# The first product of the second MoE by a seven-product scheme, for three pairs of f in its last pass

## Chip, cores and metric

One core of a Trainium2 chip runs one program that does all of the work: causal attention and two mixtures (here dense feed-forward layers, "MoE"). The metric is device time in microseconds for one execution. The core has five engines that run side by side, each taking its own instructions strictly in the order in which they were written: PE (TensorE, matrix products into PSUM), DVE (VectorE), ACT (ScalarE), POOL (GpSimd) and SP (which issues most DMAs). They wait for each other through semaphores.

## The reference, cut to what matters

```python
def reference(**kwargs):                       # S = 576, 4 batches, 8 heads of 64
    attn_out = _attn_ref(q, k, v, s)           # causal attention with a decay bias
    x = attn_out.transpose(0, 2, 1, 3).reshape(2304, 512)
    x = _moe_ref(x, w_in, w_out)               # relu(x @ w_in)**2 @ w_out
    return _moe2_ref(x, moe2_w_in, moe2_w_out)

def _moe2_ref(x, w_in, w_out):                 # x: 2304 x 512, w_in: 512 x 2048
    h = x @ w_in                               # the "first product"
    g = h * np.cos(h)
    return (g @ w_out).astype(np.float32)      # the "second product"
```

## The kernel before, in words

Everything is fp32 at the ends, and products are made from two-part numbers: each operand is split into a high part and a low part (high = the rounded value, low = what is left), and each product runs three passes (high with high, high with low, low with high; `PASSES`). Attention and the first MoE fill the first 597 us. The second MoE, which the change touches, is the rest.

The second MoE cuts the 2304 tokens into five blocks `j` (four of 512 tokens and one of 256) and the 2048 hidden columns into 16 slices `f` of 128. The loop at the end of the program goes over three passes `p` of slices, `GROUPS`: f 0 to 3, 4 to 8 and 9 to 15; in each pass over the blocks; in each block over the slices of the pass. One step (p, j, f) is called a chunk here. A chunk's work, with the helper that issues it:

- `m2_g1` (PE, L1371): the first product, 4 pieces of the 512 input columns times 3 passes = 12 matmuls of 512 columns (tokens) into one PSUM bank `hp`; each matmul has its own weight load.
- `m2_cos` (ACT L1383, then DVE L1384 and L1385): `a` = hp scaled to turns, `kf` = a rounded by adding and taking off a large number, less a.
- `m2_sin` (ACT L1392), `m2_mul` (DVE L1398: hp times the cosine), `m2_high` (ACT L1406: `gh`, the fp16 high part), `m2_rest` (L1413: `gl`, the low part; on POOL in the middle pass, on DVE otherwise).
- `m2_g2` (PE, L1426): the second product of the chunk two steps back (`G2LAG` = 2), 12 matmuls of 512 columns into four banks `o0` to `o3`. After the last slice of a pass the banks are evicted into `part`: two by DVE (L1433), two by ACT (`os`, L1438) with an addition on POOL (L1439).

The weights of the second MoE are prepared while the first two passes run: `w_clip` (ACT L804), `w_bits` (DVE L810, L814), `w_square` (ACT L847, for the scale), `w_hi` (ACT L829) and `w_lo` (DVE L838). In the middle pass one weight tile goes through per chunk, two are scaled and split in every second chunk. The tokens `y` lie in DRAM as `y_d`; `load_y` fetches 512 KB for 256 tokens. All of this is written in one fixed order per engine; nothing is reordered at run time.

Of the kernel before, what the change touches and what calls it, by code (L numbers as in the profile page):

```python
# [14 lines left out]
ALU = mybir.AluOpType  # L15
# [111 lines left out]
def attention_moe_moe_kernel(  # L127
# [679 lines left out]
    def w_bits(j):  # L807
# [8 lines left out]
        )  # L816
        yield

    def w_hi(j):
        m, f, a = wq[j]  # L820
        if m == 0:
# [6 lines left out]
        part[c] = t[:, 1]  # L828
        nc.scalar.activation(out=wt[m, f, a][:, 0], in_=wst[j][1], func=ACTF.Copy, scale=sm["wsc"][:, c:c + 1])  # L829

    def w_lo(j):
        m, f, a = wq[j]
        t, st = wt[wq[j]], wst.pop(j)[1]
# [8 lines left out]
    stat, part, sm = [], {}, {}  # L842

    def w_square(j):
        m, f, a = wq[j]
# [31 lines left out]
    def w_scale(f):  # L877

        c = slice(2 * f, 2 * f + 2)
        powers(stat[0][:, c], sm["wsm"][:, c], sm["wex"][:, c], sm["wsc"][:, c])  # L880
        for g, (f0, f1) in enumerate(GROUPS):
            if f == f1 - 1:
                group(g, f0, f1)

    def group(g, f0, f1):

        fs = slice(f0, f1)
        t, u = (sm["wsc"][:, 2 * f0 + a:2 * f1:2] for a in range(2))
        lo, il = (sm[x][:, g:g + 1] for x in ("wlo", "wil"))
        inverse(sm["win"][:, fs], t)  # L890
        nc.vector.tensor_tensor(out=sm["wtu"][:, fs], in0=t, in1=u, op=ALU.mult)
        inverse(sm["wiu"][:, fs], sm["wtu"][:, fs])
        nc.vector.tensor_reduce(out=lo, in_=sm["wtu"][:, fs], op=ALU.min, axis=mybir.AxisListType.X)
        inverse(il, lo)
        nc.vector.tensor_scalar(
            out=sm["gsc"][:, fs], in0=sm["wiu"][:, fs], scalar1=lo, scalar2=2.0 ** -16, op0=ALU.mult, op1=ALU.mult
        )
        known[0].append(g)
        for j0, j1 in known[1]:
            tables(g, j0, j1)  # L900
# [3 lines left out]
    def tables(g, j0, j1):  # L904

        fs = slice(*GROUPS[g])
        n, js = GROUPS[g][1] - GROUPS[g][0], slice(j0, j1)
        nc.vector.scalar_tensor_tensor(
            out=sm["hsc"][:, js, fs], in0=sm["win"][:, None, fs].to_broadcast([128, j1 - j0, n]),
            scalar=1.0 / (2.0 * math.pi), in1=sm["yin"][:, js, None].to_broadcast([128, j1 - j0, n]),  # L910
            op0=ALU.mult, op1=ALU.mult,
        )
        nc.vector.tensor_scalar(
            out=sm["osc"][:, g, js], in0=sm["yin"][:, js], scalar1=sm["wil"][:, g:g + 1], scalar2=2.0 ** 16,
            op0=ALU.mult, op1=ALU.mult,
        )

# [142 lines left out]
    def moe_slot():  # L1060
        part, n = slots.pop(0)
        k, f = chunks[n]
        if part == 1:
            w_need(spot[0, f, 0] + 1)
            g1(k, f)
            return n
        w_need(spot[0, f, 1] + 1)
        rests(n)
        g2(k, f)
        g2done[0] += 1  # L1070
        if k == NB1 - 1 and 2 * f >= RAWS:
            w_load(2 * (NF + f))
            w_load(2 * (NF + f) + 1)
            nw[0] = max(nw[0], 2 * (NF + f + 1))

    def act(n):
        if n is not None:
# [123 lines left out]
    def w_sums():  # L1201
        while wsum:
            m, f, a = wq[wsum[0]]
            sum_rows(2 * f + a, (sm["wss"], 2 * f + a))
            wnext.append(wsum.pop(0))

    def w_scales():
        while len(wnext) > 1:
            w_scale(wq[wnext[0]][1])
# [150 lines left out]
    hd2 = {}  # L1360
    ops = {}

    def m2_g1(j, f):
        n = blocks[j][1]
        yh, yl = yd[j]
        w = wt[1, f, 0]
        hp = ps2h.tile([128, n], F32, tag="h", bufs=3, name="hp2")
        m = 0
        for c in range(KD):
            for a, e in PASSES:  # L1370
                nc.tensor.matmul(  # L1371
                    hp, w[:, a, c * 128:(c + 1) * 128], (yh, yl)[e][:, c, :],
                    start=(m == 0), stop=(m == 3 * KD - 1),
                )
                m += 1
        hd2[j, f] = hp

    def m2_cos(j, f):
        n = blocks[j][1]
        hp = hd2[j, f]  # L1380
        a = p2.tile([128, n], F32, tag="a", bufs=2, name="a")
        kf = p2.tile([128, n], F32, tag="kf", bufs=2, name="kf")
        nc.scalar.activation(out=a, in_=hp, func=ACTF.Copy, scale=sm["hsc"][:, j, f:f + 1], bias=0.25)  # L1383
        nc.vector.tensor_scalar(out=kf, in0=a, scalar1=MAGIC, scalar2=None, op0=ALU.add)  # L1384
        nc.vector.scalar_tensor_tensor(  # L1385
            out=kf, in0=kf, scalar=MAGIC, in1=a, op0=ALU.subtract, op1=ALU.subtract
        )
        hd2[j, f] = (hp, a, kf)

    def m2_sin(j, f):  # L1390
# [57 lines left out]
    steps2 = [(p, j, f) for p, fs in enumerate(GROUPS) for j in range(NB2) for f in range(*fs)]  # L1448
    bits0 = nw[2]
    for i in range(len(steps2) + G2LAG):  # L1450
        new = i < len(steps2)
# [5 lines left out]
        if new:  # L1457
            p, j, f = steps2[i]
            w_stats(2 * NF + 2 * GROUPS[p][1])
            w_need(2 * NF + 2 * f + 2)  # L1460
            m2_g1(j, f)
            m2_cos(j, f)
        if i < G2LAG:
            m2_sin(j, f)
            m2_mul(p, j, f)
            m2_high(p, j, f)
            m2_rest(p, j, f)
        elif i <= len(steps2) and i > G2LAG:
# [81 lines left out]
```

## Time and profile before

| what | value |
|---|---|
| time, three runs | median 976.35 us (975.49 to 977.0) |
| profiled execution | span 975.0 us from first to last instruction; the runs lie 0.5 to 2.0 us above it |
| PE busy, whole span | 954.7 us (98%) |
| DVE / ACT / POOL busy | 714.3 / 656.2 / 161.9 us |
| second MoE | from about 597 us to the end |
| middle pass and last pass | about 691 to 807 us, and 807 to 971 us |

How to read it: a busy share of PE counts matmuls whose ends are modelled, so the spacing from one start to the next says more than the length of one. The same holds for DVE and ACT: an instruction's listed length reaches a little into the next one, so what a queue really spends on one is read from start to start.

### The profile page before, as it was taken

The numbers are of one execution on the slowest core, as the hardware profiler recorded it, in microseconds if no ns is written. First come the engines' busy times: TensorE is split into PE (matmuls) and PEld (weight loads), VectorE is DVE, ScalarE is ACT, GpSimd is POOL, SyncE is SP. The second block draws the span as 40 slices with busy tenths as digits, with TensorE's granted clock in tenths as the row PEclk, the third lists the DMA queues.
The fourth block names the chain that finished last, engine by engine and source line by source line (L and its number), as shares of the span: only waits on it lengthen the run. The fifth ranks groups of instructions, "written<-read, shape, count | busy, mean of one in ns | idle before, by whom it ended". The sixth has DMA issues, their size and how long they took to land.

```text
span 975.0 us, 20374 instructions
## 1 busy us (share of the span) xinstructions
PE 954.7 (98%) x7250; PEld 735.2 (75%) x7250; DVE 714.3 (73%) x1816; ACT 656.2 (67%) x1596; POOL 161.9 (17%) x251
## 2 busy tenths in 40 slices
PE   6999999999999999999999999999999999999998
PEld 5898899999999999999999996445544454444444
DVE  6899988778778777777996364888789865545555
ACT  6799877777778777776784686677558653334433
POOL 2000112111110111111110031440133430101101
PEclk9999999999999999999999999999999999999999
DMA  8974698658988865586996688200000000001101
GB/s 252 319 256 137 156 211 218 169 140 173 166 180 195 177 187 146 131 175 143 205 226 123 216 284 343 65 23 1 1 1 1 0 2 0 34 11 44 43 2 66
DMA packets 150518, 127.19 MB, mean 130 GB/s; under 512 B 107864, under 2 KB 125600, under 8 KB 150416
## 3 DMA queue, kind: packets, MB, share of 16 engines
q1 hardware_dynamic: 146512, 119.59, 47.7%
q0 software_dynamic: 3904, 6.30, 2.4%
q8 instruction: 57, 0.93, 0.4%
q14 instruction: 45, 0.37, 0.1%
HBM read 85.79 MB, written 15.83 MB: 104 GB/s over the span
## 4 chain that ended last, share of the span: by engine, by line
PE 84%; ACT 5%; DVE 5%; DMA 3%; issue 1%; POOL 1%; SPq 0%; DVEq 0%; ACTq 0%; POOLq 0%
PE hp L1371 19%; PE o L1426 19%; PE hps L942 18%; PE y L971 18%; PE qkp L557 5%; PE pvs L684 4%; DMA rw<-in_w_dram 2%; PE xps L739 1%; DVE wt L835 1%; ACT st L804 1%; ACT wt L823 1%; DVE sb L575 1%; ACT sb L598 1%; DMA v_d<-vt 0%; ACT g L954 0%
## 5 line engine op out<-in xcount | busy, mean ns | idle before, releaser
L942 PE MATMUL hps<-xh,wt 128*128 128x256 f32 x1152 | 238.9, 290 | 1.9 <-ACT g L953 1.7
L971 PE MATMUL y<-gh,wt 128*128 128x256 f32 x1152 | 236.4, 288 | 0.0
L942 PEld LDWEIGHTS hps<-xh,wt 128*128 128x128 f32 x1152 | 190.0, 192 | 4.2 <-ACT g L953 3.1
L971 PEld LDWEIGHTS y<-gh,wt 128*128 128x128 f32 x1152 | 188.8, 191 | 1.0
L1371 PE MATMUL hp<-yh,wt 128*128 128x512 f16 (+1 forms) x640 | 185.9, 358 | 0.0
L1426 PE MATMUL o<-wt,gh 128*128 128x512 f16 x576 | 171.3, 379 | 0.1
L942 PE MATMUL hps<-xl,wt 128*128 128x256 f32 x576 | 163.3, 284 | 0.2 <-DVE xl L756 0.2
L971 PE MATMUL y<-gl,wt 128*128 128x256 f32 x576 | 162.8, 283 | 0.1
L1371 PEld LDWEIGHTS <-wt 128*128 128x128 f16 x960 | 92.0, 98 | 93.0
L1383 ACT ACTIVATE a<-hp,hsc 128x512 f32<-128x512 f32 (+1 forms) x80 | 51.5, 644 | 111.3 <-PE hp L1371 109.5
L953 ACT ACTIVATE g<-hps 128x256 f32<-128x256 f32 x144 | 54.8, 380 | 102.1 <-PE hps L942 99.0
L1371 PE MATMUL hp<-yl,wt 128*128 128x512 f16 (+1 forms) x320 | 114.4, 358 | 0.0
L942 PEld LDWEIGHTS hps<-xl,wt 128*128 128x128 f32 x576 | 110.8, 192 | 0.7 <-DVE xl L756 0.4
L971 PEld LDWEIGHTS y<-gl,wt 128*128 128x128 f32 x576 | 110.1, 191 | 1.0 <-DVE gl L961 0.4
L1426 PE MATMUL o<-wt,gl 128*128 128x512 f16 x288 | 109.2, 379 | 0.0
L1426 PEld LDWEIGHTS <-gh 128*128 128x128 f16 x576 | 56.3, 98 | 64.6 <-ACT gh L1406 0.6
L1384 DVE TENSOR_SCALAR kf<-a 128x512 f32<-128x512 f32 (+1 forms) x80 | 35.7, 447 | 92.6 <-ACT a L1383 92.3
L383 POOL DMA_DIRECT2D k<-ext_d x80 | 41.1, 514 | 319.9 <-ACT g L954 102.3
L598 ACT ACTIVATE sb<-sb,nb 128x128 f32<-128x128 f32 (+7 forms) x152 | 87.6, 576 | 2.5 <-DVE nb L575 2.0
L1392 ACT ACTIVATE a<-kf 128x512 f32<-128x512 f32 (+1 forms) x80 | 46.8, 584 | 50.8 <-DVE kf L1385 50.7
L961 DVE TENSOR_TENSOR gl<-g,gh 128x256 fp32r<-128x256 f32 x144 | 60.1, 417 | 27.3 <-ACT gh L955 14.3
L575 DVE CUSTOM_DVE_ANT_0 sb<-qkp,mask 128x128 f32<-128x128 f32 (+7 forms) x152 | 69.2, 455 | 6.2 <-PE qkp L542 3.3
(124 smaller groups left out, 1681.9 us busy)
## 6 DMA issues: line engine op xcount, KB each, us to landing
rw<-in_w_dram SPq DMA_DIRECT2D x64, 512.0 KB
raw<-in_qk_dram SPq DMA_DIRECT2D x48, 352.0 KB
raw<-in_qk_dram SPq DMA_DIRECT2D x16, 384.0 KB
v_d<-vt SPq DMA_DIRECT2D x16, 320.0 KB
vb<-v_d SPq DMA_DIRECT2D x32, 160.0 KB
vr<-in_v_dram POOLq DMA_DIRECT2D x15, 320.0 KB, 5.0
y_d<-yst SPq DMA_DIRECT2D x18, 256.0 KB
yr<-y_d SPq DMA_DIRECT2D x9, 512.0 KB
```

What stands on the lines that cost most here:

```text
L383: nc.gpsimd.dma_start(out=hd[n][1][64:68, BT - nq:BT + nl], in_=ext_d[n, :, BT - nq:BT + nl])
L557: nc.tensor.matmul(p[0:r, 0:cn], m[0:kk, qo:qo + r], m[0:kk, BT + c0:BT + c0 + cn], start=(kk == 128 and not (two and h % 2)), stop=(kk == ...
L575: nc.vector.tensor_tensor_reduce(out=sb[0:r, c0:c0 + cn], in0=p[0:r, 0:cn], in1=mask[0:r, mo:mo + cn], scale=-0.125, scalar=(3.0e38 if k = ...
L598: nc.scalar.activation(out=sb[0:r, 0:w], in_=sb[0:r, 0:w], func=ACTF.Exp, scale=-1.0, bias=j["nb"], accum_out=z[0:r, ti, x:x + 1],)
L942: nc.tensor.matmul(hp, w[:, a, c * 128:(c + 1) * 128], (xh, xl)[e][:, c, :], start=(n == 0), stop=(n == 3 * KD - 1),)
L953: nc.scalar.activation(out=g, in_=hp, func=ACTF.Relu)
L961: nc.vector.tensor_tensor(out=gl, in0=g, in1=gh, op=ALU.subtract)
L971: nc.tensor.matmul(yps[k][d // 2][:, d % 2, :], w[:, a, d * 128:(d + 1) * 128], (gh, gl)[e], start=(f == 0 and n == 0 and d % 2 == 0), sto ...
L1371: nc.tensor.matmul(hp, w[:, a, c * 128:(c + 1) * 128], (yh, yl)[e][:, c, :], start=(m == 0), stop=(m == 3 * KD - 1),)
L1383: nc.scalar.activation(out=a, in_=hp, func=ACTF.Copy, scale=sm["hsc"][:, j, f:f + 1], bias=0.25)
L1392: nc.scalar.activation(out=a, in_=kf, func=ACTF.Sin, scale=-6.2831850)
L1426: nc.tensor.matmul(ops[j][a], (gh, gl)[e][:, a * 128:(a + 1) * 128], w[:, x, :], start=(first and m == 0), stop=(last and m == 2),)
```

## The change

In the last pass, for f from 10 on and the four blocks of 512 tokens, two slices f and f+1 are made together (a "unit"). The product of a 512 x 256 weight by 512 x 512 tokens is seen as a 2 by 2 by 2 product of halves (two halves of the input columns, two slices, two halves of the tokens), and instead of 8 half products it makes 7 (`PROD`), each of 2 pieces x 3 passes = 6 matmuls of 256 columns. Three PSUM banks hold running sums; what is in a bank between two products is copied out to `hs` in SBUF by ACT (`snap`) or added to `hs` by DVE (`join`).

The products need sums and differences of the operands. For the weights (`pair_high`) they are made once per pair when the weight is prepared, in the middle pass: four DVE operations on 256 columns, five pieces instead of two for high and for low parts. For the tokens (`t_make`) they are made per block, one step at each call of `t_tick`: the block is loaded from `y_d` again, four DVE differences of 512 columns, four highs on ACT, four lows on DVE. The first block's are made at the end of the middle pass (`T_FROM`), each later block's during the block before.

Besides, the rounding in `m2_cos` adds and subtracts the large number in one DVE operation and takes `a` off with a plain two-tensor operation, where before the second step did both; the order of loading the last weights follows the pairs; a scale constant is lowered by one power of two and the later factors raised to match. The block of 256 tokens and f = 9 are done as before.

```diff
+    def pair_high(j, m):
...
+        if m == 0:
+            q = p2q[0].tile([128, KD, BT], F32, tag="yr", bufs=2, name="sums")
+            x, y = (wst[j + n][1].rearrange("p (a c) -> p a c", a=2) for n in range(2))
+            for n, (u, v, op) in enumerate((
+                (y[:, 0], y[:, 1], ALU.add), (q[:, 0], x[:, 0], ALU.subtract), (x[:, 0], y[:, 0], ALU.subtract),
+                (x[:, 1], q[:, 1], ALU.subtract),
+            )):
+                nc.vector.tensor_tensor(out=q[:, n], in0=u, in1=v, op=op)
+            parts = ((t[:, :, 1:3], x), (t[:, :, 0], y[:, 1]), (t[:, :, 3], q[:, 0]))
...
+        else:
...
+            parts = ((t[:, :, 0:3], q[:, 1:4]), (t[:, :, 3], y[:, 0]))
...
+        for o, i in parts:
+            nc.scalar.activation(out=o[:, 0], in_=i, func=ACTF.Copy, scale=sc)
...
+            for o, i in parts:
+                nc.vector.scalar_tensor_tensor(
+                    out=o[:, 1], in0=i, scalar=sc, in1=o[:, 0], op0=ALU.mult, op1=ALU.subtract
+                )
...
-        nc.vector.tensor_scalar(out=kf, in0=a, scalar1=MAGIC, scalar2=None, op0=ALU.add)
-        nc.vector.scalar_tensor_tensor(
-            out=kf, in0=kf, scalar=MAGIC, in1=a, op0=ALU.subtract, op1=ALU.subtract
-        )
+        nc.vector.tensor_scalar(out=kf, in0=a, scalar1=MAGIC, scalar2=MAGIC, op0=ALU.add, op1=ALU.subtract)
+        nc.vector.tensor_tensor(out=kf, in0=kf, in1=a, op=ALU.subtract)
...
+    def unit(j, f, prev):
...
+        prod(j, f, 1, 0, True)
+        prod(j, f, 2, 1, True)
+        snap(j, f, 0, 0, 0)
+        join(j, f, 1, 0, 0)
+        out_part(first, 0)
+        for x in old:
+            m2_sin(*x[1:])
+        if old:
+            m2_mul(*old[0])
+        else:
+            m2_high(*prev[1:])
+            m2_rest(*prev[1:])
+        prod(j, f, 6, 0, False)
+        if old:
+            m2_high(*old[0])
+            m2_mul(*old[1])
+        snap(j, f, 0, 1, 0)
+        prod(j, f, 7, 2, True)
+        out_part(first, 1)
+        if old:
+            m2_high(*old[1])
+            m2_rest(*old[0])
+            m2_rest(*old[1])
+        prod(j, f, 5, 0, False)
+        snap(j, f, 0, 1, 1)
+        join(j, f, 2, 1, 1)
+        out_part(second, 0)
+        t_tick(j + 1)
+        prod(j, f, 3, 0, False)
+        snap(j, f, 0, 0, 1)
+        prod(j, f, 4, 2, False)
+        join(j, f, 2, 1, 0)
+        out_part(second, 1)
+        t_tick(j + 1)
+        for m in range(2):
+            m2_cos(j, f + m)
+            fifo.append((p, j, f + m))
```

`prod(j, f, x, b, start)` issues product x into bank b. `out_part` issues half of the second product of an earlier chunk; of the first unit in the first block there is only one such chunk (`first`), of every other unit two (`first`, `second`). `old` are the two slices of the unit before, whose cosine and split are finished inside this unit.

Three places where the order changes. The first is DVE's queue in the middle pass, where the weights of one pair are prepared. Before, after the rounding of a chunk (`kf`), the two weight tiles are finished, and then come the next tile's bits (`st`) and the chunk's own multiplication (L1398):

```order
L1385 SCALAR_TENSOR_TENSOR kf<-kf,a 128x512
L838 SCALAR_TENSOR_TENSOR wt_11405<-st,wsc,wt_11405 128x512
L838 SCALAR_TENSOR_TENSOR wt_11407<-st,wsc,wt_11407 128x512
L810 TENSOR_SCALAR st<-st 128x512
L814 SCALAR_TENSOR_TENSOR st<-rw,st 128x512
L1398 SCALAR_TENSOR_TENSOR a<-hp_11384,gsc,a 128x512
```

After the change the same place reads:

```order
L1439 TENSOR_TENSOR kf<-kf,a 128x512
L855 TENSOR_TENSOR sums<-st 128x256
L855 TENSOR_TENSOR sums<-sums,st 128x256
L855 TENSOR_TENSOR sums<-st 128x256
L855 TENSOR_TENSOR sums<-st,sums 128x256
L874 SCALAR_TENSOR_TENSOR wt_11407<-st,wsc,wt_11407 128x512
L874 SCALAR_TENSOR_TENSOR wt_11407<-st,wsc,wt_11407 128x256
L874 SCALAR_TENSOR_TENSOR wt_11407<-sums,wsc,wt_11407 128x256
L874 SCALAR_TENSOR_TENSOR wt_11416<-sums,wsc,wt_11416 128x768
L874 SCALAR_TENSOR_TENSOR wt_11416<-st,wsc,wt_11416 128x256
L813 TENSOR_SCALAR st<-st 128x512
L1450 SCALAR_TENSOR_TENSOR a<-hp_11386,gsc,a 128x512
```

Nine operations stand between `kf` and the bits, where there were two (the second bits operation, L817, stands between the last two rows shown). The second place is ACT's queue in the second unit of a block (here the second block): `hs<-bank` are the copies out of the running banks, `a<-hs` and `a<-kf` scale and sine, CAST the high part `gh`, `os` evictions, `wt<-wt` and `wt<-yr` the high parts for the next block's tokens.

```order
L1492 ACTIVATE os<-o_12342,osc 128x512 [waits PE_49]
L1520 ACTIVATE wt_9853<-wt_11300,ysc 128x512 [waits DVE_49]
L1437 ACTIVATE a<-hs,hsc 128x512 [waits Activation_49]
L1437 ACTIVATE a<-hs,hsc 128x512 [waits DVE_49]
L1581 COPY hs<-bank 128x256 [waits PE_49]
L1444 ACTIVATE a<-kf 128x512 [waits DVE_49,Activation_49] x2
L1458 CAST gh<-a 128x512 [waits DVE_49]
L1581 COPY hs<-bank 128x256 [waits PE_49]
L1458 CAST gh<-a 128x512 [waits DVE_49]
```

Before, ACT had no copies out of the banks at all in this pass; its rows for one chunk were three:

```order
L1383 ACTIVATE a<-hp_12723,hsc 128x512
L1406 CAST gh<-a 128x512
L1392 ACTIVATE a<-kf 128x512
L1383 ACTIVATE a<-hp_12763,hsc 128x512
L1406 CAST gh<-a 128x512
```

The copies now stand between the steps of the cosine, and PE waits for them. The third place is PE in that kind of unit: the first row of a product, with what it waits for (`wt_97..` and `wt_98..` right after the arrow are token tiles made by `t_make`).

```order
L1571 MATMUL bank<-wt_9719,wt_11623 128x256 [waits Activation_49]
L1571 MATMUL bank<-wt_9853,wt_11623 128x256 [waits DVE_49]
...
L1571 MATMUL bank<-wt_9717,wt_11614 128x256 [waits Activation_49]
L1480 MATMUL o_12310<-wt_11511,gh 128x512
L1480 LDWEIGHTS gl [waits DVE_49]
...
L1571 MATMUL bank<-yh,wt_11623 128x256 [waits Activation_49]
L1571 MATMUL bank<-wt_9855,wt_11614 128x256 [waits DVE_49]
```

Before, a chunk's twelve matmuls of the first product went one after the other into one bank without such waits.

## Rows read from the trace of the kernel before

**Rows 1.** Head of the page.
```profile
span 975.0 us, 20374 instructions
```

**Rows 2.** Busy time in one stretch: PE, PEld, DVE, ACT, POOL, granted clock, DMA.
```profile
737.00:747.00 10.00, 10.00 (x50) 4.53 (x48) 9.68 (x17) 8.10 (x16) 2.55 (x3) 1.00 0.00 1
```

**Rows 3.** Timeline of one chunk in the last pass: start, length, engine, line, operation [idle].
```profile
851.36 0.59 PE L1426 MATMUL o<-wt,gh 128*128 128x512 f16 x2
851.56 0.69 ACT L1383 ACTIVATE a<-hp,hsc 128x512 f32<-128x512 f32 x1 [1.43 <-PE hp L1371]
852.14 0.61 ACT L1406 CAST gh<-a 128x512 f16<-128x512 f32 x1
852.28 0.43 DVE L1384 TENSOR_SCALAR kf<-a 128x512 f32<-128x512 f32 x1 [1.45 <-ACT a L1383]
852.74 0.69 DVE L1385 SCALAR_TENSOR_TENSOR kf<-kf,a 128x512 f32<-128x512 f32 x1
853.35 0.68 DVE L1413 TENSOR_TENSOR gl<-a,gh 128x512 f16<-128x512 f32 x1
853.95 0.38 PE L1371 MATMUL hp<-yh,wt 128*128 128x512 f16 x1
```

**Rows 4.** Timeline of one chunk of the block of 256 tokens.
```profile
950.87 1.41 PEld L1371 LDWEIGHTS <-wt 128*128 128x128 f16 x12
951.09 0.27 PE L1371 MATMUL hp<-yh,wt 128*128 128x256 f16 x1
...
952.40 0.59 PE L1426 MATMUL o<-wt,gh 128*128 128x512 f16 x2
952.60 0.47 ACT L1383 ACTIVATE a<-hp,hsc 128x256 f32<-128x256 f32 x1 [1.85 <-PE hp L1371]
...
953.43 0.43 DVE L1385 SCALAR_TENSOR_TENSOR kf<-kf,a 128x256 f32<-128x256 f32 x1
...
953.77 0.42 DVE L1413 TENSOR_TENSOR gl<-a,gh 128x256 f16<-128x256 f32 x1
```

**Rows 5.** Timeline of DVE in the middle pass, where weights are split.
```profile
732.00 1.60 DVE L1385 SCALAR_TENSOR_TENSOR kf<-kf,a 128x512 f32<-128x512 f32 x1
733.53 1.40 DVE L838 SCALAR_TENSOR_TENSOR wt<-st,wsc,wt 128x512 f16<-128x512 f32 x2
...
736.08 0.75 DVE L1398 SCALAR_TENSOR_TENSOR a<-hp,gsc,a 128x512 f32<-128x512 f32 x1
...
763.25 1.64 DVE L838 SCALAR_TENSOR_TENSOR wt<-st,wsc,wt 128x512 f16<-128x512 f32 x2 [0.59 <-ACT wt L829]
...
771.92 0.43 DVE L1384 TENSOR_SCALAR kf<-a 128x512 f32<-128x512 f32 x1 [0.89 <-ACT a L1383]
```

**Rows 6.** Timeline of POOL there.
```profile
731.90 1.16 POOL L1413 TENSOR_TENSOR gl<-a,gh 128x512 f16<-128x512 f32 x1 [2.40 <-ACT gh L1406]
737.56 1.35 POOL L1413 TENSOR_TENSOR gl<-a,gh 128x512 f16<-128x512 f32 x1 [4.50 <-ACT gh L1406]
...
757.83 1.34 POOL L1413 TENSOR_TENSOR gl<-a,gh 128x512 f16<-128x512 f32 x1 [4.51 <-ACT gh L1406]
```

**Rows 7.** Timeline of PE there: the matmuls at three points where PE could wait.
```profile
740.14 0.38 PE L1426 MATMUL o<-wt,gl 128*128 128x512 f16 x1
...
760.96 0.38 PE L1426 MATMUL o<-wt,gl 128*128 128x512 f16 x1
...
776.79 0.59 PE L1426 MATMUL o<-wt,gh 128*128 128x512 f16 x2
```

**Rows 8.** Timeline of ACT at the third pair's place: highs, two evictions.
```profile
772.92 1.32 ACT L829 ACTIVATE wt<-st,wsc 128x512 f16<-128x512 f32 x2
...
774.66 1.25 ACT L1438 ACTIVATE os<-o,osc 128x512 f32<-128x512 f32 x2
```

**Rows 9.** Two DVE lines, 690 to 970 us: shortest/median/longest ns, span of starts.
```profile
L1385 DVE SCALAR_TENSOR_TENSOR kf<-kf,a x60: 424/692/1602, 691.7 to 967.8; 128x512 f32<-128x512 f32 x48, 128x256 f32<-128x256 f32 x12
L1398 DVE SCALAR_TENSOR_TENSOR a<-hp,gsc,a x61: 473/746/752, 690.3 to 968.7; 128x512 f32<-128x512 f32 x48, 128x256 f32<-128x256 f32 x13
```

More of the change, by code (lines that the diff above doesn't have):

```diff
@@ L817, in w_bits, with split @@
         yield
+    def split(j):
+        return wq[j][0] == 1 and wq[j][1] >= PAIR0 and wq[j][2] == 0
+    pair = {}
     def w_hi(j):
         m, f, a = wq[j]
+        if split(j):
+            pair_high(j, f % 2)
+            return
         if m == 0:
@@ L840, in w_lo @@
         )
-    stat, part, sm = [], {}, {}
+    stat, part, half, sm = [], {}, {}, {}
     def w_square(j):
@@ L1070, in moe_slot @@
         g2done[0] += 1
[L1071 to L1074, printed above, removed]
+        if k == NB1 - 1 and 2 * f >= RAWS and not (f >= PAIR0 and f % 2 == 0):
+            while nw[0] < 2 * (NF + f + 1):
+                w_load(nw[0])
+                nw[0] += 1
     def act(n):
@@ L1446, in m2_g2, with t_make, minus, high @@
                     nc.sync.dma_start(out=out[row:row + m, :], in_=part[4 * j + a][x:x + m])
-    steps2 = [(p, j, f) for p, fs in enumerate(GROUPS) for j in range(NB2) for f in range(*fs)]
-    bits0 = nw[2]
-    for i in range(len(steps2) + G2LAG):
-        new = i < len(steps2)
+    HB = BT
+    PROD = {1: (0, 1, 0), 2: (0, 2, 1), 3: (1, 2, 2), 4: (0, 0, 6), 5: (0, 3, 3), 6: (1, 0, 4), 7: (1, 1, 5)}
+    yt = {}
+    def t_make(j):
+        to = [half[4 * (j % 2) + x].bitcast(F16).rearrange("p (e c h) -> p e c h", e=2, c=2) for x in range(4)]
+        ysc = sm["ysc"][:, j:j + 1]
+        load_ys(j)
+        yield
+        r, q = (yr[j, a] for a in range(2))
+        t3 = part[18].rearrange("p (c h) -> p c h", c=2)
+        src = (r[:, 0:2], q[:, 2:4], t3, r[:, 2:4])
+        def minus(o, x, y):
+            nc.vector.tensor_tensor(out=o, in0=x, in1=y, op=ALU.subtract)
+        def high(x):
+            nc.scalar.activation(out=to[x][:, 0], in_=src[x], func=ACTF.Copy, scale=ysc)
+        def low(x):
+            nc.vector.scalar_tensor_tensor(
+                out=to[x][:, 1], in0=src[x], scalar=ysc, in1=to[x][:, 0], op0=ALU.mult, op1=ALU.subtract
+            )
+        minus(src[2], q[:, 2:4], q[:, 0:2])
+        yield
+        high(2)
+        minus(src[0], q[:, 0:2], r[:, 0:2])
+        yield
+        high(0)
+        low(2)
+        minus(src[1], q[:, 2:4], src[0])
+        yield
+        high(1)
+        low(0)
+        minus(src[3], r[:, 2:4], src[1])
+        yield
+        high(3)
+        low(1)
+        yield
+        low(3)
+        yt[j] = to
@@ new lines, in attention_moe_moe_kernel, with t_tick, y_side, prod @@
+    now2 = [0, t_make(0)]
+    def t_tick(j):
+        while now2[0] <= min(j, NB2 - 2):
+            if next(now2[1], now2) is not now2:
+                return
+            now2[0] += 1
+            now2[1] = t_make(now2[0])
+    def y_side(j, x, e, c):
+        if x < 3:
+            return yd[j][e][:, c + 2 * (x > 0), HB * (x == 2):HB * (x == 2) + HB]
+        return yt[j][x - 3][:, e, c]
+    bank = {}
+    def prod(j, f, x, b, start):
+        m, wx, yx = PROD[x]
+        w = pair[f][m]
+        if start:
+            bank[b] = ps2h.tile([128, 2 * HB], F32, tag="h", bufs=3, name="bank")
+        n = 0
+        for c in range(2):
+            for a, e in PASSES:
+                nc.tensor.matmul(
+                    bank[b][:, 0:HB], w[:, a, wx, c * 128:(c + 1) * 128], y_side(j, yx, e, c),
+                    start=(start and n == 0), stop=(n == 5), skip_group_check=True,
+                )
+                n += 1
@@ new lines, in piece, with snap, join, out_part @@
+    def piece(j, f, m, t):
+        return hd2[j, f + m][:, t * HB:(t + 1) * HB]
+    def snap(j, f, b, m, t):
+        nc.scalar.copy(piece(j, f, m, t), bank[b][:, 0:HB])
+    def join(j, f, b, m, t):
+        o = piece(j, f, m, t)
+        nc.vector.tensor_tensor(out=o, in0=bank[b][:, 0:HB], in1=o, op=ALU.add)
+    fifo = []
+    def out_part(x, n):
+        if x is not None:
+            k = blocks[x[1]][1] // 128 // 2
+            m2_g2(*x, pick=range(n * k, n * k + k))
+    def unit(j, f, prev):
+        p = len(GROUPS) - 1
+        w_need(2 * NF + 2 * f + 4)
+        while now2[0] <= j:
+            t_tick(j)
+        first = fifo.pop(0) if len(fifo) != 2 or prev[0] != "u" else None
+        second = fifo.pop(0) if len(fifo) > 1 else None
+        for m in range(2):
+            hd2[j, f + m] = stq[0][0].tile([128, 2 * HB], F32, tag="stg", bufs=4, name="hs")
+        old = [prev[1:], (prev[1], prev[2], prev[3] + 1)] if prev[0] == "u" else []
+        prod(j, f, 1, 0, True)
[32 more added lines that the diff above has]
+        t_tick(j + 1)
+        for m in range(2):
+            m2_cos(j, f + m)
+            fifo.append((p, j, f + m))
@@ L1452, in attention_moe_moe_kernel @@
+    bits0 = nw[2]
+    prev = None
+    for i, (kind, p, j, f) in enumerate(items):
+        if kind == "u":
+            unit(j, f, prev)
+            prev = (kind, p, j, f)
+            continue
         if i >= QUIET:
@@ L1500, in attention_moe_moe_kernel @@
             y_sums(NB2 - 1, NB2)
+        if i >= T_FROM:
+            t_tick(0 if p < 2 else j + 1)
+        fifo.append((p, j, f))
+        prev = (kind, p, j, f)
+    m2_high(*prev[1:])
+    m2_rest(*prev[1:])
+    while fifo:
+        m2_g2(*fifo.pop(0))
 def _lay_out(inputs):
```

128 lines of the change are left out of this document (83 added, 45 removed).

## The prediction, as it was put on record before the changed kernel was run

> **What bounds the kernel now.** I read the span first [rows 1], then the busy time by stretch, then the timeline of a chunk. The second MoE is bound by PE: in ten microseconds of its middle pass PE is busy for all ten, at the full granted clock of 2.4 GHz [rows 2], and in the last pass the twelve matmuls of a second product start at 851.36 and the next chunk's first at 853.95, that is 2.59/12 = 0.216 us from start to start [rows 3]. So a chunk costs PE 24 x 0.216 = 5.19 us, and what shortens PE's list shortens the kernel, as long as nothing makes PE wait. The reader should see a second thing in [rows 2]: DVE is at 9.68 of 10 us there. It is a hair from being the bound of the middle pass, and the change adds to it just there.
>
> **What the change takes away.** Twelve units (three pairs in four blocks) replace 24 matmuls of 512 columns by 42 of 256. The price of 256 columns is read in the last block: twelve start at 951.09, the next matmul at 952.40, so 1.31/12 = 0.109 us each [rows 4]. A unit's first product goes from 24 x 0.216 = 5.19 to 42 x 0.109 = 4.59 us. Saved: 0.60 us, times 12 = **7.2 us**, if PE never waits.
>
> **New waits in the last pass.** Durations are from start to start, which is shorter than the listed length: ACT on 512 columns 0.58, DVE `kf` 0.46 and 0.61 [rows 3]; DVE on 256 columns with two inputs 0.34 [rows 4]; a DVE eviction or low about 0.66 to 0.70, half of two in 1.40 [rows 5]. From PE's last start plus its column time to ACT's start is 0.20 us (952.40 plus nothing to 952.60, [rows 4]); I take 0.13 us from an ACT or DVE end to its reader. The copy of a bank (256 columns out of PSUM on ACT) is not in the trace: below it 0.33, half a 512-column step and a start cost, above it the 0.47 listed for L1383 [rows 4]; I take 0.37, the start-to-start value that the 512-column row suggests, and 0.40 for the addition from a bank on DVE (between 0.34 and 0.43).
>
> Three kinds of wait follow.
> - In the very first unit only one chunk is at hand for the second product, so product 3 follows product 5 into the same bank at once: 0.20 + 0.37 + 0.13 = 0.70 us.
> - In the second unit of blocks 1 and 2 the queues arrive late. The unit before has carried the evictions of the previous block and the first token differences. Counted from the start of product 1: ACT still has an eviction copy (0.20 to 0.79), a high part (to 1.39) and two scalings (to 2.55), so the copy of bank 0 ends at 2.92 and product 6, which could start at 2.61, starts at 3.05: 0.44. DVE can begin the four `kf` steps only with the first scaling (1.97 + 0.13, a POOL addition pushes it to 2.17) and ends them at 4.27, then a bank addition (4.67) and the first multiplication (5.28); ACT's CAST, 5.43 to 5.95, stands ahead of the copy of product 6, 5.95 to 6.32. Product 5 could start at 5.66 and starts at 6.45: 0.79. Together 1.23 in each of two blocks.
> - The second unit of block 0 (no eviction) 0.24, that of block 3 (no new tokens to make, but the POOL additions) 1.23, and 0.04 at one more start.
>
> Sum 0.70 + 2 x 1.23 + 0.24 + 1.23 + 0.04 = **4.7 us** back. From below only the 0.70 is certain; from above, with 0.05 more on each copy, addition and low, 5.3, and 6.5 if the third units wait as well. The third units run free in this table, since DVE has caught up by then.
>
> Part of that sum is a matter of ports. L1398 read the product from PSUM and never took over 752 ns in 61 runs; L1385, with both inputs in SBUF, took up to 1602 [rows 9], as at 732.00, while a POOL operation ran from 731.90 for 1.16 us [rows 5, 6]. With `hs` in SBUF the multiplication joins the second kind. I count 1.0 of the 4.7 us for waits behind the POOL additions. The Trainium skill (SBUF — State Buffer, "Who interferes with whom") says that a DVE instruction with two SBUF inputs contends with a GpSimd instruction that reads SBUF and one of the two blocks fully. The trace agrees (1602 against 752 ns); without the rule the waits would sum to 3.7.
>
> The new rounding I put at nothing: its second step, a two-tensor operation, occupies DVE like the one before (0.61 for L1385; L1413, also two SBUF inputs, is listed at 0.68 against 0.69, [rows 3]), and its first is one pass over the same columns. If the first step lost its speed it would take about 0.6 instead of 0.46, and then the middle pass would lose more (case D). The second loading of `y` is issued a whole chunk before its first reader and PE has 5.2 us of other work; I price it at nothing, and 1 to 2 us once if DVE stands waiting for the first block's.
>
> **New waits in the middle pass.** DVE's queue gets, per pair, four operations of 256 columns (4 x 0.34 = 1.36 us) and five lows in place of two. The two took 1.40 [rows 5]; the five are one of 512 (0.66), three of 256 (3 x 0.35) and one of 768 (0.9, the 512-column value plus half of it less the start), 2.6 together. Per pair 1.36 + 2.6 - 1.40 = 2.6 us more. ACT's five highs are 1.2 us more and wait for the sums; they lie beside DVE's lows. Everything queued behind on DVE comes later by 2.6 us: the next bits and the chunk's multiplication, hence CAST, POOL's `gl` and PE's second product.
> - First pair, at 733.53: POOL's `gl` runs 737.56 to 738.91, PE reads it at 740.14 [rows 6, 7]: 1.2 us of slack. 2.6 - 1.2 = 1.4 us of waiting.
> - Second pair, two chunks times two later: DVE has had no idle time in between (9.68 of 10, [rows 2]), so its lateness is 5.2 us. `gl` runs 757.83 to 759.17, PE reads it at 760.96: slack 1.8. PE is then 5.2 - 1.8 = 3.4 us late in all, so 2.0 more.
> - Third pair: DVE's idle 0.59 and 0.89 us [rows 5] bring its lateness down to about 3.7, near PE's own 3.4. Here ACT's eviction decides. It began at 774.66, and bank 1 was free at about 775.2, 1.6 us before PE's 776.79 [rows 7, 8]. Now it stands behind DVE's sums (1.36) and longer highs (1.2), with 0.1 for the hand-over, on a queue 0.2 later than PE: 2.9 - 1.6 = 1.3; `gl` behind the POOL additions loses no more. I take 1.1.
>
> Sum 1.4 + 2.0 + 1.1 = **4.5 us**. From below 0, if DVE's waits for POOL fall elsewhere (the 0.9 us that L1385 lost at 732.00 recurs at most chunks) and free the 2.6 us; from above 3 x 2.6 = 7.8, all of it exposed.
>
> **The sum.** -7.2 + 4.7 + 4.5 = +2.0 us. The profiled execution's span is 975.0, the median 976.35: 977.0 and **978.3**. A measurement of this kernel can tell about 0.2% (1.95 us) from no change, so under 974.4 is faster and over 978.3 slower: the forecast sits on that edge.
>
> **The rivals.**
> - B, faster: DVE's lateness in the middle pass stays covered. For: POOL's waits eat nearly 1 us per chunk and may fall differently, and the slack of 1.2 to 2.5 us is counted per chunk. Against: no idle time in [rows 2]. It decides at 1.2 us: if a pair adds less than that before DVE recovers, nothing shows. Then 976.35 - 7.2 + 4.7 = 973.9.
> - C, no change: half of the middle-pass waits, 976.35 - 7.2 + 4.7 + 2.3 = 976.2.
> - D, clearly slower: DVE carries the extra work fully exposed, 976.35 - 7.2 + 4.7 + 7.8 = 981.7. For: DVE is at 97%. Against: the idle 0.59 and 0.89 us at the third pair.
> - E, the change does not do what it says, because 256 columns do not pay: weight loads bind. The loads of twelve such matmuls take 1.41 us, as long as the matmuls [rows 4]. From 5.19/42 = 0.124 us per matmul on, nothing is saved. At 0.141 us, if loads and matmuls with new addresses hid a quarter less, a unit would cost 5.9 and twelve 16 us more than counted: 994. Against: 0.109 measured in the same alternation. Beside it, the Trainium skill (TensorE: Matmul & The Clock Gate, "Back-to-back issue gap") gives about 131 ns for 512 columns and 81 for 128 in a stream with weight loads, by which narrow matmuls cost more than their share; the trace disagrees, with 216 for 512 and 109 for 256.
>
> **How the numbers follow.** Forecast and its near values (976.5 to 980.5) 0.45, B 0.25, C 0.13, D 0.15, E 0.02. Of the first case half lies within 0.2%. Faster: B, 0.26 with tails. Same: C and some 0.17 of the first, 0.30. Slower: the rest of the first, D and E, 0.44. The range 973.3 to 982.0 reaches from B to D and leaves out about 2 in 10; the likeliest case alone is 976.5 to 980.5.
>
> **What would show it.** In the changed profile: matmuls of 256 columns in the running banks 0.109 us apart; PE idle ahead of L1571 released by ACT copies (L1581), about 1.2 us in the second unit of a block and none in the third; PE idle ahead of L1480 in the middle pass, in three places 20 us apart, released by POOL's `gl` and, at the third, by `os`; DVE without a gap from the first pair to the second. Wrong if the middle pass keeps its length (then B), if its waits exceed 6 us (D), if the units wait at other places than the second, or if the spacing is above 0.115.

## The result, and the profile of the changed kernel

The changed kernel takes 983.8 us (median of 4 runs, 982.73 to 985.56) against 976.5 before (975.49 to 977.0): ratio 1.0077, 95% interval 1.0062 to 1.0091, that is 7.3 us slower. The prediction said 978.3, in a range of 973.3 to 982.0. The profiled execution has a span of 982.0 where [rows 1] have 975.0.

Where do the 7.0 us lie? The last pass begins with the first 512-column product after the block of 256 tokens. The timeline of PE in the kernel before shows that place:

```profile
803.33 0.27 PE L1371 MATMUL hp<-yh,wt 128*128 128x256 f16 x1
...
804.74 0.38 PE L1371 MATMUL hp<-yh,wt 128*128 128x512 f16 x1
```

and the timeline of PE in the changed kernel:

```profile
813.32 0.27 PE L1426 MATMUL hp<-yh,wt 128*128 128x256 f16 x1
...
814.72 0.38 PE L1426 MATMUL hp<-yh,wt 128*128 128x512 f16 x1
```

From there to the end it was 975.0 - 804.74 = 170.26 us and is 982.0 - 814.72 = 167.28: the last pass gained 3.0 us (forecast 7.2 - 4.7 = 2.5). What comes ahead lost 10.0; at 711.09 (before) and 710.44 (after), early in the middle pass, the changed kernel was still 0.65 us ahead, so the middle pass lost 10.6 us, where 4.5 was forecast and 7.8 was the upper bound. (The 0.65 us are no effect of the change: the second MoE's first matmul starts at 596.73 before and at 596.08 after, and between 595.11 and 597.78 in the runs below.) Measured from its own first 512-column product to that of the last pass, the middle pass was 116.98 us and is 127.62; the experiments are compared by this length too. The busy time of the changed kernel by stretch, columns as in [rows 2]:

```profile
740.00:750.00 10.00, 9.18 (x47) 4.13 (x46) 9.71 (x17) 8.04 (x17) 3.10 (x3) 1.00 0.00 1
...
760.00:770.00 10.00, 8.21 (x30) 3.09 (x29) 9.68 (x18) 7.97 (x15) 2.50 (x2) 0.83 0.17 52
...
780.00:790.00 10.00, 7.93 (x37) 3.16 (x36) 9.14 (x14) 5.58 (x10) 4.65 (x3) 1.00 0.16 54
...
800.00:810.00 10.00, 8.88 (x60) 5.48 (x57) 9.32 (x15) 5.20 (x12) 5.00 (x4) 1.00 0.00 0
```

and the last of these stretches in the kernel before:

```profile
800.00:810.00 10.00, 10.00 (x59) 5.53 (x57) 4.88 (x10) 3.92 (x10) 2.61 (x4) 1.00 0.01 2
```

PE, which stood at 10 of 10 in [rows 2] and has no wait at all from 690 us on in the kernel before, has holes around 740, 763, 785 and from 800 on; the first three are the places of the three pairs. In 760 to 770 the granted clock is 0.83. DVE is at 9.7 of 10 in the first two stretches shown and at 9.1 and 9.3 in the later two; from 800 to 810, where the block of 256 tokens runs, that is nearly twice the 4.88 of before. The waits of PE from 690 us to the end, in total, times, longest:

```profile
PE o L1480 <- POOL gl L1465: 3.4, 4, 0.9
PE bank L1571 <- ACT hs L1581: 3.2, 7, 1.0
PE o L1480 <- ACT gh L1458: 1.6, 3, 1.0
PE o L1480 <- DVE wt L1487: 1.1, 1, 1.1
PE o L1480 <- ACT os L1492: 1.0, 1, 1.0
```

A wait costs more than the idle time shown, because that is counted from the listed end of the matmul ahead, and a matmul is listed 0.38 us long where the next starts after 0.216; from start to start it is about 0.17 us more. The timeline of PE at the waits in the middle pass:

```profile
738.88 0.38 PE L1426 MATMUL hp<-yh,wt 128*128 128x512 f16 x1
739.62 0.60 PE L1480 MATMUL o<-wt,gh 128*128 128x512 f16 x2 [0.36 <-ACT gh L1458]
741.05 0.39 PE L1480 MATMUL o<-wt,gl 128*128 128x512 f16 x1 [0.82 <-POOL gl L1465]
...
761.28 0.38 PE L1426 MATMUL hp<-yh,wt 128*128 128x512 f16 x1
762.64 0.60 PE L1480 MATMUL o<-wt,gh 128*128 128x512 f16 x2 [0.98 <-ACT gh L1458]
764.06 0.39 PE L1480 MATMUL o<-wt,gl 128*128 128x512 f16 x1 [0.82 <-POOL gl L1465]
...
764.72 0.51 PE L1480 MATMUL o<-wt,gl 128*128 128x512 f16 x1
765.02 1.06 PE L1480 MATMUL o<-wt,gh 128*128 128x512 f16 x2
765.88 0.64 PE L1480 MATMUL o<-wt,gl 128*128 128x512 f16 x1
...
768.35 0.59 PE L1426 MATMUL hp<-yh,wt 128*128 128x512 f16 x2
...
782.87 0.59 PE L1480 MATMUL o<-wt,gh 128*128 128x512 f16 x2 [0.99 <-ACT os L1492]
...
787.85 0.61 PE L1480 MATMUL o<-wt,gh 128*128 128x512 f16 x2 [0.26 <-ACT gh L1458]
789.27 0.39 PE L1480 MATMUL o<-wt,gl 128*128 128x512 f16 x1 [0.82 <-POOL gl L1465]
...
807.13 0.59 PE L1480 MATMUL o<-wt,gh 128*128 128x512 f16 x2 [1.12 <-DVE wt L1487]
...
811.24 0.39 PE L1480 MATMUL o<-wt,gl 128*128 128x512 f16 x1 [0.92 <-POOL gl L1465]
```

Read it as a bill. First pair: 738.88 + 0.216 = 739.10 to 739.62, and 739.62 + 2 x 0.216 = 740.05 to 741.05: 1.5 us. Second pair, in the same way: 1.1 + 1.0 = 2.1 us. Right behind it two matmuls take 0.86 us from start to start (765.02 to 765.88) in place of 0.43: PE had stood idle for 0.98 and 0.82 us, and its clock fell to the lower level, 1.2 GHz, until 768.35. The busy time of one microsecond in between, with the granted clock at 0.50:

```profile
766.00:767.00 1.00, 1.00 (x4) 0.33 (x3) 0.96 (x3) 1.00 (x4) 0.59 (x1) 0.50 0.00 0
```

The nine matmuls from 764.72 to 768.35 take 3.63 us in place of 9 x 0.216 = 1.94: **1.7 us** more. Third pair: 1.2 at the eviction's copy, and 1.4 in the next chunk. In the 256-token block 1.12 + 0.92 and twice 0.17: 2.4. Sum 1.5 + 2.1 + 1.7 + 1.2 + 1.4 + 2.4 = 10.3 of the 10.6 us.

In the last pass the narrow matmuls run as forecast, twelve from 818.61 to 819.92, 0.109 each, and the waits stand ahead of L1571. The timeline of PE and ACT in the second unit of block 1:

```profile
863.07 1.47 PE L1571 MATMUL bank<-wt,wt 128*128 128x256 f16 x12 [0.26 <-ACT hs L1581]
865.43 0.62 ACT L1458 CAST gh<-a 128x512 f16<-128x512 f32 x1 [0.30 <-DVE a L1450]
865.46 0.38 PE L1480 MATMUL o<-wt,gl 128*128 128x512 f16 x1
865.95 0.37 ACT L1581 COPY hs<-bank 128x256 f32<-128x256 f32 x1
866.37 0.82 PE L1571 MATMUL bank<-wt,wt 128*128 128x256 f16 x6 [0.53 <-ACT hs L1581]
```

Product 6 waits 0.26 + 0.17 = 0.43 (forecast 0.44), product 5 from 865.46 + 0.216 to 866.37, 0.69 (forecast 0.79), behind a copy that stands behind a CAST. All seven waits: 3.2 + 7 x 0.17 = 4.4 us, forecast 4.7.

### The profile page after: what moved, and what is told of

It is laid out like the page before. It is cut to its first block, busy times and chain, and to the rows that moved or that the text cites. A ratio compares the mean times of both kernels' runs of the same rounds, so it can differ in the third digit from the quotient of the medians.

```text
span 982.0 us, 20976 instructions
## 1 busy us (share of the span) xinstructions
PE 951.3 (97%) x7472; PEld 755.7 (77%) x7472; DVE 762.3 (78%) x1905; ACT 687.9 (70%) x1669; POOL 162.2 (17%) x251
## 4 chain that ended last, share of the span: by engine, by line
PE 74%; DVE 10%; DMA 7%; ACT 5%; issue 3%; POOL 1%; SPq 0%; DVEq 0%; ACTq 0%; POOLq 0%
PE y L1017 18%; PE hps L988 18%; PE o L1480 14%; PE hp L1426 9%; DMA rw<-in_w_dram 6%; PE bank L1571 5%; PE qkp L560 5%; PE pvs L687 4%; DVE kf L1439 1%; DVE a L1450 1%; PE xps L742 1%; DVE kf L1438 1%; DVE st L817 1%; DVE wt L874 1%; DVE wt L880 1%
## 5 line engine op out<-in xcount | busy, mean ns | idle before, releaser
L1426 PE MATMUL hp<-yh,wt 128*128 128x512 f16 (+1 forms) x448 | 125.2, 349 | 0.0
L1426 PEld LDWEIGHTS <-wt 128*128 128x128 f16 x672 | 64.2, 98 | 59.6 <-issue 1.0
L1426 PE MATMUL hp<-yl,wt 128*128 128x512 f16 (+1 forms) x224 | 78.2, 349 | 0.0
L642 DVE TENSOR_SCALAR p<-sb 128x384 f16<-128x384 f32 (+3 forms) x120 | 43.2, 360 | 39.5 <-ACT sb L601 21.2
L646 DVE SCALAR_TENSOR_TENSOR p<-sb,p 128x384 f16<-128x384 f32 (+3 forms) x120 | 66.4, 553 | 3.8 <-DVE p L642 0.2
```

Source lines behind the costliest of these rows:

```text
L646: nc.vector.scalar_tensor_tensor(out=p[0:r, cw:cw + w], in0=sb[0:r, 0:w], scalar=PSC, in1=p[0:r, 0:w], op0=ALU.mult, op1=ALU.subtract,)
L1426: nc.tensor.matmul(hp, chunk_of(w, a, c), (yh, yl)[e][:, c, :], start=(m == 0), stop=(m == 3 * KD - 1),)
```

## The experiments

Every version keeps the whole computation. In the texts that were put down ahead, VectorE is DVE, ScalarE ACT, GpSimd POOL and TensorE PE. The first four runs divide the change.

**r1_rounding**: the kernel before, with the two new lines for `kf`.

```diff
-        nc.vector.tensor_scalar(out=kf, in0=a, scalar1=MAGIC, scalar2=None, op0=ALU.add)
-        nc.vector.scalar_tensor_tensor(
-            out=kf, in0=kf, scalar=MAGIC, in1=a, op0=ALU.subtract, op1=ALU.subtract
-        )
+        nc.vector.tensor_scalar(out=kf, in0=a, scalar1=MAGIC, scalar2=MAGIC, op0=ALU.add, op1=ALU.subtract)
+        nc.vector.tensor_tensor(out=kf, in0=kf, in1=a, op=ALU.subtract)
```

> The kernel before with one edit, the rounding of the changed kernel (add and subtract in one tensor_scalar, then one tensor_tensor). Theory, VectorE over its capacity in the middle pass through the pairs' preparation: no change, 976.5 within 0.7 us, since the two operations took 434 and 792 ns in the changed kernel against 474 and 803 before. Rival, the rounding itself makes every chunk's kf late: slower by 2 us or more.

Measured 975.99, ratio 0.9997 (0.9986 to 1.0008). The rounding costs nothing. (The expectation's 434 and 474 ns are means over different stretches. Over the same one, from 690 us on, the first step took 442 ns on average in this run and 442 in the kernel before.)

**r2_no_pairs**: the changed kernel without its units.

```diff
-PAIR0 = 10
-T_FROM = 36
+PAIR0 = 16
+T_FROM = 1000
```

> The changed kernel without pairs and without token differences (PAIR0 = 16, T_FROM never reached): what is left of the change is the rounding, the scale, the order of the code of the last passes. Theory (VectorE, pairs): 976 to 977. Rival, the rewritten order of the loop or the rounding costs: 978 or more.

Measured 976.13, ratio 0.9999 (0.9990 to 1.0008). The rewritten loop costs nothing either.

**r3_prep_plain** and **r4_pairprep_plain**: all preparation, but plain products in the last pass.

```diff
-        n = PAIR0 if j < NB2 - 1 else NF
+        n = NF
...
-            t_tick(0 if p < 2 else j + 1)
+            t_tick(0)
```

(r4 has `T_FROM = 1000` in place of the second edit.)

> The changed kernel with the three pairs and the first block's token differences prepared as before, but the last pass takes plain products in every block, and the differences of the later blocks are not made. Theory (the middle pass lost about 10.6 us, the units gained about 3): 976.5 + 10.6 = 987, and the last pass as long as before. Rival, the preparation costs the 4.5 us that were forecast and the units cost the rest: 981.

> As the run with the preparation and plain products, but without any token differences (T_FROM never reached), so that only the three pairs' sums and halves are added to the middle pass. Theory: 976.5 + 8 = 984.5, since about 2.4 of the 10.6 us stood beside the first block's token differences. Rival, the three pairs cost 4.5 as forecast and what is over it comes from the token differences: 981.

Measured r3 985.93, ratio 1.0108 (1.0084 to 1.0131), and r4 983.93, ratio 1.0082 (1.0067 to 1.0098): by the ratios 10.5 and 8.0 us over before. So the three pairs' preparation alone costs about 8 (the bill above: 1.5 + 2.1 + 1.7 + 1.2 + 1.4 = 7.9). Both intervals exclude the rival's 981 (ratio 1.005). What the first block's token differences cost (r3 against r4) and what the units win back (r3 against the changed kernel) is 2 to 3 us each; there the intervals overlap, and the traces decide. The middle pass is 127.62 us in r3, as in the changed kernel, and 125.13 in r4, that is 2.5 less, and PE's waits in r4 are only

```profile
PE o L1480 <- POOL gl L1465: 2.5, 3, 0.8
PE o L1480 <- ACT gh L1458: 1.6, 3, 1.0
PE o L1480 <- ACT os L1492: 1.0, 1, 1.0
```

without the two in the 256-token block (1.12 and 0.92 us). The last pass is 170.65 us in r3 and 170.32 in r4, against 167.28 with the units. The fall of the clock is there again in both; the busy time of r4:

```profile
760.00:770.00 10.00, 8.21 (x30) 3.08 (x29) 9.79 (x17) 7.87 (x16) 2.50 (x2) 0.83 0.00 0
```

The next four ask what about the pairs costs.

**v1_no_pause**:

```diff
-        goal = min(4 * NF, bits0 + int(max(0, min(k, PAUSE)) * P_BITS) + max(0, k - PAUSE - 5))
+        goal = min(4 * NF, bits0 + int(max(0, min(k, PAUSE)) * P_BITS) + max(0, k - PAUSE))
```

> The changed kernel, its weights' preparation without the pause of five chunks, so that each pair is prepared about 26 us earlier and the stretch from 690 to 727, where VectorE is 7 to 8 tenths busy, takes a share. Theory A, what counts is VectorE's load over the whole middle pass: the waits fall by half or more, 979 to 981. Theory B, what counts is the 4.2 us burst of one pair in one chunk's time, whenever it comes: the pairs' 7.5 us stay, 983 to 984.

Measured 980.73, ratio 1.0048 (1.0033 to 1.0063): about 3 us won, in the range of theory A, but not in its way. By the traces the middle pass is 2.9 us shorter (124.73): PE's idle time in it fell only from 7.1 to 6.3 us, where theory A has half or more, and 1.7 us is the clock, which stays at 1.00 in every stretch. The waits moved: the largest is now one of 1.67 us at 700.44 for an ACT eviction, in the stretch that was free before, and from 770 to 780 DVE is busy for 3.65 of 10.

**v2_burst_split**:

```diff
             while wrest:
                 w_rest(wrest.pop(0))
+                if split(wlow[-1]):
+                    break
```

(and `w_step` leaves a pair for the next chunk's time.)

> The changed kernel with each pair's burst split: sums and first lows in one chunk's time, second lows (1.4 us) in the next; the order of the weights stays. Theory B (burst): two thirds of the pairs' waits go, 978 to 980. Theory A (load): the load is the same, 982 to 984.

Measured 986.16, ratio 1.0103 (1.0088 to 1.0118): slower than both theories allow. The timeline of DVE, SP's queue and PE shows a third thing:

```profile
788.14 0.47 DVE L874 SCALAR_TENSOR_TENSOR wt<-st,wsc,wt 128x256 f16<-128x256 f32 x1
788.24 0.32 SPq L1057 DMA_DIRECT2D yr<-y_d  x1
...
792.66 0.69 DVE L1517 TENSOR_TENSOR wt<-yr 128x512 f32<-128x512 f32 x1 [3.39 <-DMA yr<-y_d]
...
798.80 0.86 PE L1480 MATMUL o<-wt,gh 128*128 128x512 f16 x2 [2.52 <-ACT gh L1458]
```

The pair's sums live in one of the two `yr` buffers into which `y` is loaded again. Held a chunk longer, they let the load start only at 788.24; DVE stands for 3.39 us in front of the first token difference, and PE for 2.52 behind it. Behind that wait the clock falls too (0.95 from 790 to 800, 0.88 from 800 to 810). This run does not tell the theories apart.

**v3_gl_on_vector**:

```diff
-        (nc.gpsimd if p == 1 else nc.vector).tensor_tensor(out=gl, in0=a, in1=gh, op=ALU.subtract)
+        nc.vector.tensor_tensor(out=gl, in0=a, in1=gh, op=ALU.subtract)
```

> The changed kernel with the middle pass's gl on VectorE in place of GpSimd. In the trace of the changed kernel the shift L813 took 1.38 us beside a gl of GpSimd and 0.42 without one, while a gl on VectorE takes 0.6: theory C, GpSimd's gl costs VectorE more (0.97) than it saves (0.6), and the waits for GpSimd's gl (3.4 us in four) go: 979 to 981. Rival: 0.6 us more of VectorE in each chunk makes its lateness worse: 985 or more.

Measured 979.45, ratio 1.0034 (1.0022 to 1.0047): 4.3 us won. The shift L813 in 690 to 790 us, shortest/median/longest ns, in the changed kernel:

```profile
L813 DVE TENSOR_SCALAR st<-st x14: 415/1379/1386, 699.5 to 772.6; 128x512 int32<-128x512 int32 x14
```

and in this run:

```profile
L813 DVE TENSOR_SCALAR st<-st x14: 419/421/1495, 700.7 to 773.2; 128x512 int32<-128x512 int32 x14
```

with, among PE's waits,

```profile
PE o L1480 <- DVE gl L1465: 1.8, 5, 0.4
```

A shift that met POOL's `gl` took 0.96 us longer. The Trainium skill (SBUF — State Buffer, "Who interferes with whom") says that a `tensor_scalar` within SBUF can take the port pair that DVE shares with GpSimd, and that the later of two instructions then blocks fully; the trace agrees (1379 against 421 ns). Still DVE as a whole is not less busy (9.6 of 10 from 760 to 770, 9.7 from 790 to 800): that part of theory C is not borne out. What went is the way over POOL, a wait of 0.8 us each for its `gl`, now at most 0.4 for DVE's, and the fall of the clock, which stays at 1.00 here. PE's idle time in the middle pass is 3.9 us in place of 7.1; these 3.2 and the clock's 1.7 are about what the middle pass is shorter by, 123.04 us against 127.62.

**v4_all_three**: v1, v2 and v3 together.

> The three edits together (no pause, split burst, gl on VectorE). If each takes its share away, the middle pass loses under 2 us and the units' gain of 2 to 3 us shows: 974 to 977. If VectorE has no room left at all: 981 or more.

Measured 979.69, ratio 1.0038 (1.0023 to 1.0053): a miss, no better than v3. New waits, 1.5 us for an ACT eviction and 1.3 for a statistics operation of DVE, stand where the work went. Which of the two other edits eats the gain, this run leaves open.

The last four use what was seen: the bursts have to fall between the chunks that are short or carry evictions, and the token differences ahead of the 256-token block.

**b1_early**, **b2_early_snap**, **b3_two_pairs**: `gl` on DVE as in v3, and

```diff
-T_FROM = 36
+T_FROM = 34
...
-        goal = min(4 * NF, bits0 + int(max(0, min(k, PAUSE)) * P_BITS) + max(0, k - PAUSE - 5))
+        goal = min(4 * NF, bits0 + int(max(0, min(k, PAUSE)) * P_BITS) + max(0, k - PAUSE - 2))
```

b2 and b3 also

```diff
+        snap(j, f, 0, 1, 0)
         if old:
             m2_high(*old[0])
             m2_mul(*old[1])
-        snap(j, f, 0, 1, 0)
```

and b3 `PAIR0 = 12`, two pairs.

> The changed kernel with gl of the middle pass on VectorE, the pause shortened from five chunks to two, so that no pair's burst falls into a chunk with evictions or into the short 256-token chunks, and the first block's token differences begun two chunks earlier (T_FROM = 34), so that five of their eight steps lie before the 256-token block. Theory (VectorE's load and where its bursts fall): the middle pass loses about 2 us, 976 to 978. If the order within the middle pass is worth nothing beyond the place of gl: 979.5 as with gl alone.

> The same, and in a unit ScalarE's copy of product 6's bank (L1581) stands ahead of the cast of the earlier chunk. In the last pass TensorE waited 3.1 us in six places for such copies, up to 1.0 each at product 5, where the copy stood behind a cast that waits for VectorE. Theory, those waits are ScalarE's order: 1 to 2 us less than without this edit. Rival, the cast comes late instead and the second product waits for it: no difference.

> The same as the run with the copy moved, but with two pairs (PAIR0 = 12) in place of three: 8 units in place of 12. If the middle pass now costs nothing more, the missing pair's units cost their gain, 4 x 0.6 = 2.4 us less their own waits: 1 to 2 us slower than with three pairs. If each pair still costs its 1 to 3 us of waits: the same or faster.

Measured b1 976.57, ratio 0.9995 (0.9986 to 1.0005); b2 974.68, ratio 0.9983 (0.9974 to 0.9993); b3 973.65, ratio 0.9972 (0.9962 to 0.9983). The place of the work alone takes the changed kernel's whole loss away: in b1 the middle pass is 120.69 us long. How much of this the earlier pairs and how much the earlier token differences do was not tried apart. Moving the copy is worth 1.9 us (the last pass goes from 166.97 to 165.01 us, the middle pass stays); PE's waits from 660 us on in b1 and b2 show that it is the wait meant:

```profile
PE bank L1571 <- ACT hs L1581: 3.1, 6, 1.0
```

```profile
PE o L1480 <- DVE gl L1465: 1.2, 3, 0.4
PE bank L1571 <- ACT hs L1581: 1.1, 3, 0.5
PE o L1480 <- ACT gh L1458: 0.8, 1, 0.8
PE o L1480 <- ACT os L1492: 0.5, 1, 0.5
```

In b3 they are

```profile
PE bank L1571 <- ACT hs L1581: 0.5, 1, 0.5
PE o L1480 <- DVE gl L1465: 0.4, 1, 0.4
PE o L1480 <- ACT gh L1458: 0.3, 1, 0.3
```

Of the two expectations for b3 the second holds: the third pair pays no more than it costs (2.5 us of waits in the middle pass in b2, 0.7 in b3, for 2.4 us of narrow products). By the traces it costs 2.4 us of the middle pass (120.67 against 118.27) and wins 0.9 in the last (165.01 against 165.93). That b3 is faster than b2 the intervals do not show, but it is faster than both the kernel before and the changed one.

**c1_no_pairs_early**: b3's order with the constants of r2 (`PAIR0 = 16`, `T_FROM = 1000`).

> The two-pair version without its pairs and token differences (PAIR0 = 16, T_FROM never reached): gl of the middle pass on VectorE and the shorter pause stay. If the pairs carry the 2.9 us by which the two-pair version is faster than before: the same as before, 976 to 977. If the place of gl and the pause carry it: 973 to 975.

Measured 975.92, ratio 0.9996 (0.9986 to 1.0006): without pairs that order, with `gl` on DVE, is worth nothing. The 2.9 us of b3 come from the scheme.

## Why the prediction was wrong, point by point

- **What bounds the kernel**: right. PE's spacing held everywhere, except where its clock fell.
- **What the change takes away, 7.2 us**: right; 0.109 us per narrow matmul, and rival E (weight loads bind) is refuted.
- **New waits in the last pass, 4.7 us**: right in the places, first and second units, and near in sum (4.4), the sum in part by luck. In the first unit product 3 waited 0.46 + 0.17 = 0.63, forecast 0.70; the second units of blocks 1 to 3 waited 1.1 to 1.2 each, forecast 1.23. The first unit also waited 0.32 ahead of product 6, which was not forecast, and the second unit of block 0 did not wait, where 0.24 was. Of the 1.0 us that was counted for waits behind the POOL additions, the multiplication had no part: all 24 multiplications with `hs` took 741 to 752 ns, and none ran beside a POOL operation, so whether they collide no run shows.
- **The rounding at nothing**: right, shown by r1_rounding.
- **New waits in the middle pass, 4.5 us**: the step that failed. The three named waits came at their places and by their releasers: 1.4, 2.0, 1.1 forecast, 1.5, 2.1, 1.2 measured. The first two are right in mechanism: DVE's work on the first pair ran from 732.87 to 737.11, 4.24 us where 1.36 + 2.6 were counted. The size of the third is luck. The timeline of POOL and DVE there:

```profile
777.32 1.62 POOL L1465 TENSOR_TENSOR gl<-a,gh 128x512 f16<-128x512 f32 x1 [3.66 <-ACT gh L1458]
777.84 1.38 DVE L855 TENSOR_TENSOR sums<-st 128x256 f32<-128x256 f32 x1
```

The first sum, beside POOL's `gl`, took 1.38 us in place of 0.41 at the first pair, so the four ended at 780.27, 1.1 us later than counted. In return, ACT's first two highs ran beside the sums (from 777.77), where the forecast put the whole 1.2 us of longer highs behind them. The two errors nearly cancel. The step left out two things altogether. PE's own clock: behind the second pair's waits it fell to 1.2 GHz for 1.7 us of loss. And the third pair's lateness in the next chunk, 1.4 us: `gl` "loses no more", the prediction said, but the last lows ran beside POOL's additions (3.30 us from 782.89) and took 2.03 and 1.49 us where 0.9 and 0.35 were counted. The timeline of DVE and POOL in the changed kernel:

```profile
782.89 3.30 POOL L1493 TENSOR_TENSOR wt<-os,wt 128x512 f32<-128x512 f32 x2 [3.95 <-ACT os L1492]
783.04 2.03 DVE L874 SCALAR_TENSOR_TENSOR wt<-sums,wsc,wt 128x768 f16<-128x768 f32 x1
784.99 1.49 DVE L874 SCALAR_TENSOR_TENSOR wt<-st,wsc,wt 128x256 f16<-128x256 f32 x1
```

- **The token differences of the first block, priced at nothing** (beside the load of `y`): wrong by 2.4 us, shown by the traces of r3 and r4. The load was indeed no wait in the changed kernel; the eight operations on DVE were not priced at all. The later ones fall into chunks of 256 columns, in which PE needs less time and DVE has the least room: in 800 to 810 DVE goes to 9.32 of 10, one eviction comes 1.12 us late, and the `gl` that POOL makes behind its additions 0.92.
- **The rivals**: the run went the way of D (981.7) and past it, not by its mechanism: the first pair's 2.6 us were not exposed whole; the rest came from the clock, POOL and the token differences. By the spans the forecast missed 7.0 - 2.0 = 5.0 us: 6.1 in the middle pass, of which the three terms it left out are 1.7 + 1.4 + 2.4 = 5.5, less the 0.5 that the last pass did better and the 0.65 ahead of the second MoE. The clock alone does not decide the miss: the one run of the changed kernel whose mean granted clock is 1.0 took 982.73.

## What to carry to other kernels

Where the bound engine has no slack, price every operation that a change adds to an engine which is 97% busy, also the ones that come once, in the chunk in which they fall; a short chunk has the least room. An idle stretch of the bound engine can cost its clock on top. The same preparation cost the middle pass 10.6 us or 3.7 (b1: 120.69 - 116.98), depending on which engine and which chunks it fell to: when a scheme pays in one stage and loses in another, move its preparation before giving it up, and take only as many pairs as the preparing stage has room for.

## What the runs showed of the hardware that was not expected

- Behind two waits of PE, 0.98 and 0.82 us with two matmuls between, its clock fell to 1.2 GHz: matmuls of 512 columns 0.43 us apart in place of 0.216 from 764.72 to 768.35 (granted 0.83 over 760 to 770), in three kernels at the same place. In v2_burst_split it fell behind a wait of 2.52 us. In v1_no_pause PE waited 0.97 and 0.81 us in the same way, at 738.84 and 740.26, and the clock stayed at 1.00; it did there behind a single wait of 1.67 us as well. The mean granted clock of the four runs is 0.998, 1.0, 0.998 and 0.998 for the changed kernel and 0.998, 1.0, 1.0 and 0.998 for r4, so the fall seems not to come in every execution of the same kernel. The length of the waits does not decide it alone; what does was not tried.
- An add and a subtract in one `tensor_scalar` take as long as the add alone (442 ns on average for 512 columns in r1_rounding, 442 in the kernel before, both from 690 us on).
- Lows of 768 and 256 columns took 2.03 and 1.49 us beside POOL additions of two SBUF inputs; the same low of 256 columns took 0.48 at 736.72, with POOL idle.
